# The join of block inverses in 64x64 array tiles over zeroed rows, with all steps in a new order

## The chip, the core and the metric

The kernel runs on one core of one Trainium2 chip. The metric is the device time of one execution in microseconds. The profile shows the core's engines: PE (TensorE, matrix products, with its weight loads as PEld), DVE (VectorE), ACT (ScalarE), POOL (GpSimd) and SP (which issues DMAs). Each engine works through its own queue in the order in which the program put the instructions there, and waits at an instruction until what it needs is done.

## The reference

A recurrent attention block (RWKV-7) on 4 batches, 8 heads, 768 steps and 40 dimensions feeds an exact GELU layer (3072 tokens, 320 to 2048 to 320):

```python
for t in range(S):
    y[:, :, t] = np.einsum('bhd,bhde->bhe', rt, state)
    Sa = np.einsum('bhde,bhe->bhd', state, at)
    state_decay = state * wt[:, :, None, :] - np.einsum('bhd,bhe->bhde', Sa, bt)
    state = state_decay + np.einsum('bhd,bhe->bhde', vt, kt)
...
h = x @ w_in
g = 0.5 * h * (1.0 + erf(h * inv_sqrt2))
return (g @ w_out).astype(np.float32)
```

The weights `w_in` and `w_out` come in float64 and are converted on the core.

## The kernel before, in words

The 768 steps are cut into 12 chunks `c` of 64 steps. There are 32 pairs of a batch and a head; two heads of 64 rows fill 128 partitions, and a state of 16 such units `n` is handled at once. Within a chunk the recurrence is solved with matrix products: the strictly triangular 64x64 matrix `N` of each unit has to be inverted (as I - N), and the inverse `Tt` is applied to the right-hand sides.

The inverse is made of blocks of 32 (`BL`). For chunk 0 it is done by repeated squaring on PE (`qm.0` to `qm.4`, with `qc`, `qz`, `qb`, `qa` on ACT and DVE between them); `qm.1` to `qm.4` multiply `both_ZT[half(q), n]`, 64 rows and 64 columns, into rows `half(q)`, where `half(q)` are the partitions 0 to 63 or 64 to 127. For the chunks 1 to 11 the two diagonal blocks are inverted on POOL: `nd` and `nx` bring the blocks into `Nb`, `iz` sets the start, `ic.c.j0.j1` does the elimination, step by step, with two POOL operations each (L961, L963), and `wx` (DVE, L932) brings the result into the right halves of the columns of `Tt`; `wa` (ACT, L937) copies the upper block's inverse to the left half. Then the two block inverses are joined by two products of 32x32 blocks: `tc_` transposes the upper block's inverse, `jm` multiplies it with the block of `N` between the two, `jc` (ACT, L1091) copies the result out of PSUM, `km` multiplies it with the lower block's inverse, and `kt0`, `kt1` (L1116) copy this into `Tt`. [...]

What uses the inverse: `av` and `xm` make the right-hand sides, `xc0`, `xc1` copy them, `sm` multiplies with `Tt`, `sc` masks, `pk` and `pb` make the products for the new state and the outputs, `oa`, `od`, `om` (DVE) add and scale them, `oc`, `ot`, `tn` turn the state for the next chunk, `ym` and `yc` use it there. `om` writes the rows of the chunk's output into `xt`, and `ox.c.0`, `ox.c.1` (DMA on SP's queue) move the rest of them across partitions. With `xt` complete, `mh.c.0` to `mh.c.7` are the products with `w_in` (L1309, 64x64 tiles, four of them in turn), `ge` the GELU, and for chunks 1 to 11 the second layer is done by seven products `m1` to `m7` with sums and differences `s1` to `s4`, `e1` to `e6` (a Strassen step; L1348). Other steps that the prediction names: `nm`, `am`, `vm` are the products that make `N` and its neighbours (L193, four 64x64 tiles), `cu` sums of logarithms, `sk` and `sb` scalings, `Ls` and `Lf` the loads of the weights, `warm` and `warm_first` products whose result nobody reads.

The order is written out by hand or by a search, in one string of step names in `order` (about 1450 of them): `perform` calls the steps in this order, and each step puts its instructions at the ends of the queues of its engines. So the string fixes the order in every queue, SP's with the DMAs too, and every wait follows from it. All matrix products that go through the helper `mm` carry its line, L193.

PSUM is held in four banks of [128, 2, 512]; `take` and `drop` hand them out in order.

Of the kernel before, what the change touches and what calls it, by code (L numbers as in the profile page):

```python
# [18 lines left out]
def order(chunks, first_seven):  # L19
    return """  # L20
        first_ones.1 Lw.1 stripes_set identity pads_extra.1 sums_mask Lw.0 pads_r.1 warm.4.20 upper_mask
        pads_extra.3 La.0 pads_a.1 warm.4.0 pads_VR.1 pads_VR.0 of_half_set Lb.0 bias_set warm.4.13 pads_r.0 lg.1
        first_ones.0 pads_w.0 pads_rows.0 warm.4.25 pads_extra.0 Lb.1 pads_rows.1 onward_set lg.0 pads_w.1 wT.1
        pads_a.0 pads_extra.2 La.1 wT.0 warm.4.2 ew.1 Lf.0.1.0 ta.0 Lf.1.1.0 cu.0 Lf.0.0.0 cu.1 ec.0 Lf.1.0.0
        ew.0 sb.0 tb.0 sa.0 Lk.0 warm.4.15 sn.0 ec.1 nm.0 sb.1 Lf.2.0.0 warm_set tb.1 nk.0 Lf5.0.0 ta.1 sn.1 qt
        parity_set iz.1 sa.1 qm.0 qi.0.p qi.1.v nm.1 qz.0 warm_first ce.1 Lf.3.0.0 nk.1 qb.0.0.v Lf.3.1.0 qc.0
        cs.1 qb.0.1.a nd.1 qm.1 sk.0.p ce.0 nx.1 Lr.0 cm.1 Tt_zero tk.0 cs.0 cn.1 ic.1.0.4 qc.1 Lf.2.1.0 cl.1
        cx.1 qz.1 kc.0 Lf5.0.1 qb.1.0.v qa.1 qb.1.1.a cm.0 cy.1 ic.1.4.8 qm.2 Lf.0.0.1 cv.0 ce.3 LV.0 warm.4.18
        qz.2 am.0 qb.2.0.v qa.2 cs.3 ic.1.8.12 tr.0 Lf.1.0.1 ce.2 ak.0 Lw.2 qb.2.1.a cs.2 qc.2 Lf.0.1.1 rc.0 qm.3
        Lk.1 ic.1.12.16 Lf.2.0.1 qa.3 qz.3 Lf5.1.1 tv.0 qb.3.0.v qb.3.1.a cm.3 cm.2 cv.3 qm.4 vc.0 ic.1.16.20  # L30
# [5 lines left out]
        mh.0.0 nk.2 ot.0.1 cg.6 ot.0.0 ak.1 Ls.1 nd.2 Ls.0 nx.2 mh.0.1 iz.2 ce.8 tn.0 LV.2 unused.a mh.0.2 wb.1
        cs.8 ic.2.0.4 Lk.2 cm.8 cv.8 ge.0.0 av.1 Ls.6 ce.11 ym.1 ce.10 cs.11 ic.2.4.8 Ls.5 mh.0.3 tc_.1 Lr.2
        cm.11 yc.1 sk.2.v xm.1 cs.10 Ls.7 ge.0.1 cm.10 tv.2 ic.2.8.12 Ls.9 xc1.1 cv.10 xc0.1 Ls.10 jm.1 vc.2
        cv.11 Ls.8 tr.2 ce.12 tk.2 Ls.11 mh.0.6 ce.13 cs.12 ic.2.12.16 La.3 cm.12 kc.2 cs.13 mh.0.7 wa.1.1 cm.13
        jc.1 cv.12 rc.2 am.2 vm.2 cv.13 ic.2.16.20 ce.14 pm.0.0 Ls.13 cl.14 cs.14 Ls.12 ce.15 cm.14 ak.2 Lw.3  # L40
        cn.14 cs.15 km.1 wa.1.0 cg.14 vk.2 pm.0.1 kt1.1 ta.3 kt0.1 Ls.15 cm.15 Ls.14 cv.15 ic.2.20.24 ce.16 Lbt.3
        sm.1 ge.0.3 cs.16 ce.17 mh.0.4 sc.1.0 Lwt.3 sc.1.1 cl.17 ic.2.24.28 cm.16 mh.0.5 cs.17 Lr.3 cm.17 lg.3
        cv.16 pk.1 cn.17 cg.17 pb.1 ge.0.2 oa.1.0 cu.3 Lk.3 oa.1.1 pm.0.3 ec.3 od.1.0 Lw.4 ic.2.28.31 od.1.1 oc.1
        tw.3 ot.1.0 om.1.1 sk.3.p ot.1.1 om.1.0 av.2 tn.1 ox.1.1 pc.0.1 lt.3 ym.2 wx.2 iz.3 pm.0.2 tc_.2 yc.2
        unused.r pw.3 so.0.1 ew.3 tb.3 ox.1.0 jm.2 wb.2 en.3 pc.0.0 xm.2 jc.2 sn.3 km.2 xc0.2 tr.3 mh.1.0 xc1.2
# [5 lines left out]
        tk.4 m7.1 ic.3.24.28 e4.1 LV.4 tb.4 m4.1 e5.1 Lr.5 ic.3.28.31 xm.3 e6.1 pw.4 so.1.1 mh.2.6 xc0.3 La.5
        wx.3 ew.4 tc_.3 cu.4 sb.3 jm.3 en.4 so.1.0 mh.2.7 wb.3 sn.4 Lv.4 wa.3.0 jc.3 xc1.3 wa.3.1 km.3 sa.4 ec.4
        mh.2.4 sk.4.p tr.5 ge.2.3 kt1.3 Lkt.5 iz.4 ta.5 kt0.3 nm.4 sm.3 nk.4 Lw.5 mh.2.5 nd.4 nx.4 sc.3.0
        ic.4.0.4 mh.2.2 sc.3.1 Lbt.5 tv.4 mh.2.3 ic.4.4.8 kc.4 Lb.4 pk.3 ge.2.1 Lwt.5 ge.2.2 tb.5 pb.3 mh.2.0
        ic.4.8.12 sb.4 oa.3.1 oa.3.0 mh.2.1 od.3.0 om.3.1 am.4 ge.2.0 ic.4.12.16 om.3.0 vm.4 od.3.1 ox.3.1 m1.2
        s1.2 lg.5 tw.5 oc.3 ot.3.0 m2.2 s2.2 s4.2 m5.2 Lv.5 e1.2 vk.4 lt.5 ic.4.16.20 ot.3.1 s3.2 m6.2 ox.3.0
        ak.4 pw.5 m3.2 e3.2 ew.5 m7.2 La.6 e2.2 ic.4.20.24 tn.3 en.5 e4.2 m4.2 e5.2 av.4 e6.2 tk.5 so.2.1
        ic.4.24.28 ym.4 sn.5 Lr.6 mh.3.6 yc.4 sa.5 tv.5 LV.5 xm.4 ic.4.28.31 cu.5 xc1.4 xc0.4 mh.3.7 ec.5 wx.4
        tc_.4 wa.4.1 iz.5 ta.6 nm.5 ge.3.3 vm.5 Lbt.6 tr.6 wb.4 jm.4 nk.5 mh.3.2 jc.4 nd.5 Lwt.6 wa.4.0 nx.5
        mh.3.3 kc.5 ic.5.0.4 Lkt.6 vk.5 km.4 ge.3.1 mh.3.0 kt1.4 ic.5.4.8 kt0.4 tb.6 La.7 am.5 sm.4 tw.6  # L60
# [1408 lines left out]
```

## Time and profile before

| | |
|---|---|
| median of 3 runs | 650.9 us (650.2 to 651.37) |
| the profiled execution | 648.82 us, span 646.9 us |
| PE busy | 617.4 us, 95% |
| DVE, POOL, ACT busy | 457.3, 379.6, 323.9 us |
| mean granted PE clock | 0.991 |

The span is from the first to the last instruction; some 2 us lie around it. "Busy" of PE is modelled, since its products are pipelined: the time that a group of products takes is better read from its start to the start of the next. A matrix product of the program appears as two records, each with its load of weights. A row of the profile gives the line, engine, operation, the tiles written and read, the array tile (rows*columns) and the size, the count, busy time and mean, and the idle time of the engine just before, with what ended it.

### The profile page before, as it was taken

What the parts mean: (1) busy time and instruction counts of PE and PEld (TensorE: products, weight loads), DVE (VectorE), ACT (ScalarE), POOL (GpSimd) and SP (SyncE); (2) the same over time, 40 slices, a digit from 0 to 9 for tenths busy, and PEclk for the clock granted to TensorE, in tenths of its full rate; (3) what the DMA queues carried; (4) which work ended last, traced back from release to release, by engine and by line L of the source; (5) the groups of instructions that cost most, each with busy time, mean ns of one, the idle gap of its engine ahead of it and who ended that gap; (6) DMA issues with size and microseconds to landing.
All of it is one profiled execution on the core that took longest, in us unless ns stands there. A gap on an engine that the chain in (4) does not pass through costs nothing.

```text
span 646.9 us, 31736 instructions
## 1 busy us (share of the span) xinstructions
PE 617.4 (95%) x14338; PEld 530.9 (82%) x14338; DVE 457.3 (71%) x557; ACT 323.9 (50%) x456; POOL 379.6 (59%) x782
## 2 busy tenths in 40 slices
PE   7798999989999999998999999999998999999997
PEld 4576886768988988977887998988986987989977
DVE  0889889869887987884977876975883874843313
ACT  4467797863462564733644436463572466042021
POOL 4388289707855857848948548858704867910000
PEclk9799999989999999999999999999999999999999
DMA  8998586757477358384538346348447124110100
GB/s 132 183 174 153 119 187 165 133 107 131 98 137 135 63 101 151 77 136 86 110 80 149 65 96 113 70 88 143 94 74 128 25 48 89 38 28 4 32 13 20
DMA packets 246914, 64.31 MB, mean 99 GB/s; under 512 B 228380, under 2 KB 243644, under 8 KB 246780
## 3 DMA queue, kind: packets, MB, share of 16 engines
q1 hardware_dynamic: 246340, 62.01, 51.2%
q8 instruction: 112, 1.84, 1.3%
q10 hardware_dynamic: 440, 0.29, 0.2%
q14 instruction: 22, 0.18, 0.1%
HBM read 54.39 MB, written 3.93 MB: 90 GB/s over the span
## 4 chain that ended last, share of the span: by engine, by line
PE 74%; issue 2%; ACT 2%; DVE 1%; DVEq 0%; ACTq 0%
PE bank L1309 29%; PE bank L1348 26%; PE bank L193 18%; DVE kT L721 0%; ACT L1314 0%; ACT L734 0%; ACT spare L922 0%; ACT T L942 0%; ACT Tt L937 0%; DVE spare L864 0%; ACT wpT L734 0%; ACT st L1194 0%; ACT kT L738 0%; ACT gt L1314 0%; DVE Tt L932 0%
## 5 line engine op out<-in xcount | busy, mean ns | idle before, releaser
L1309 PE MATMUL bank<-xt,w_in_sb 64*64 64x256 f32 x3840 | 224.5, 379 | 6.7 <-issue 6.0
L961 POOL TENSOR_TENSOR tmp<-W,Nb 128x126 f32<-128x126 f32 (+22 forms) x341 | 162.8, 478 | 95.3 <-DVE Nb L927 69.7
L1309 PEld LDWEIGHTS bank<-xt,w_in_sb 64*64 64x64 f32 x3840 | 161.3, 133 | 52.0 <-issue 11.1
L963 POOL TENSOR_TENSOR W<-W,tmp 128x126 f32<-128x126 f32 (+22 forms) x341 | 169.0, 496 | 26.7
L1348 PE MATMUL bank<-w_out_sb,gt 128*128 128x160 f32 x704 | 101.1, 301 | 0.0
L1314 ACT ACTIVATE gt<-bank 128x1024 f32<-128x1024 f32 x48 | 48.8, 1025 | 99.5 <-PE bank L1309 99.4
L1348 PEld LDWEIGHTS bank<-w_out_sb,gt 128*128 128x128 f32 x704 | 96.6, 190 | 2.3 <-issue 1.3
L1175 DVE TENSOR_TENSOR SM<-bank,upper 128x832 f32<-128x832 f32 (+1 forms) x24 | 23.0, 988 | 27.0 <-PE bank L193 25.8
L1263 ACT COPY conv<-st 32x128 f32<-32x128 f32 (+2 forms) x55 | 28.0, 510 | 17.6 <-DVE st L1257 15.9
L1227 DVE TENSOR_TENSOR st<-bank,st 128x832 f32<-128x832 f32 (+1 forms) x22 | 21.2, 986 | 14.4 <-PE bank L193 14.4
L1299 DVE TENSOR_TENSOR conv<-gt 128x1024 f32<-128x1024 f32 x11 | 14.1, 1280 | 24.3 <-ACT gt L1314 24.2
L1348 PE MATMUL bank<-extra,conv 128*128 128x160 f32 x208 | 30.3, 300 | 0.0
L1299 DVE TENSOR_TENSOR os<-os,bank 128x160 f32<-128x160 f32 x44 | 13.8, 314 | 21.8 <-PE bank L1348 20.1
L1348 PEld LDWEIGHTS bank<-extra,conv 128*128 128x128 f32 x208 | 28.9, 190 | 0.1
L721 DVE TENSOR_TENSOR_SCAN kT<-spare,kT 128x256 f32<-128x256 f32 x36 | 25.5, 766 | 0.8 <-ACT kT L714 0.7
L1348 PE MATMUL bank<-extra,gt 128*128 128x160 f32 x176 | 25.8, 300 | 0.0
L1348 PEld LDWEIGHTS bank<-extra,gt 128*128 128x128 f32 x176 | 24.5, 190 | 0.1
L789 POOL TENSOR_TENSOR bk_rows<-bk_rows,part 128x640 f32<-128x640 f32 x9 | 14.9, 1659 | 15.0 <-ACT part L742 13.4
L193 PE MATMUL bank<-SM,Tt 64*64 64x104 f32 (+1 forms) x768 | 20.6, 248 | 1.8 <-issue 1.5
L193 PEld LDWEIGHTS bank<-SM,Tt 64*64 64x64 f32 x768 | 19.0, 133 | 3.7 <-issue 2.3
L1314 ACT ACT_TABLE_LOAD x17 | 21.8, 1283 | 0.3
L1348 PE MATMUL bank<-extra,SM 128*128 128x160 f32 x144 | 21.2, 300 | 0.0
(220 smaller groups left out, 1117.5 us busy)
## 6 DMA issues: line engine op xcount, KB each, us to landing
bk_rows<-in_b_dram SPq DMA_DIRECT2D x24, 160.0 KB
bk_rows<-in_k_dram SPq DMA_DIRECT2D x24, 160.0 KB
out_dram<-os SPq DMA_DIRECT2D x46, 80.0 KB
VR<-in_v_dram SPq DMA_DIRECT2D x22, 160.0 KB
w_tile<-in_w_dram SPq DMA_DIRECT2D x36, 80.0 KB
a_pairs<-in_a_dram SPq DMA_DIRECT2D x18, 144.0 KB
a_pairs<-in_b_dram SPq DMA_DIRECT2D x18, 144.0 KB
v_pairs<-in_w_dram SPq DMA_DIRECT2D x18, 144.0 KB
```

The source lines that it names most:

```text
L193: nc.tensor.matmul(o, lhsT, rhs, start=first, stop=True, skip_group_check=True)
L721: nc.vector.tensor_tensor_scan(logs[:, at:at + n], onward, logs[:, at:at + n], 0.0, ALU.mult, ALU.add)
L789: (nc.vector if q == "v" else nc.gpsimd).tensor_tensor(to, rows(k_of(c)), decays(c), ALU.mult)
L961: nc.gpsimd.tensor_tensor(t, W[:, BL // 2 - rows:, rest:rest + 1].to_broadcast([P, rows, rest]), Nb[:, rest:rest + 1, :rest].to_broadcast( ...
L963: nc.gpsimd.tensor_tensor(own, own, t, ALU.add)
L1175: nc.vector.tensor_tensor(SM[:, g, :, :, cols], pair_of(f"S{c}_", g).rearrange("p x i c -> p i x c")[:, :, :, cols], kept, ALU.mult)
L1227: nc.vector.tensor_tensor(to, pair_of(f"QY{c}_", g)[:, :, :, cols], to, ALU.add)
L1263: nc.scalar.copy(apart.rearrange("p e i g d -> p (e i g) d")[to_rows, :, to_col:to_col + n], st.rearrange("p e i g c -> p (e i g) c")[rows ...
L1299: nc.vector.tensor_tensor(to, one_, other, how)
L1309: nc.tensor.matmul(ph[half(x ^ y), x, s], w_in_sb[half(x), kt, at:at + HP], xt[half(x), kt], start=kt == 0, stop=kt == NK - 1, skip_group_ ...
L1314: nc.scalar.activation(gt[:, 4 * q:4 * q + 4].rearrange("p (x s) t -> p x s t", x=2), bank(f"ph{c}_{q}").rearrange("p x (s t) -> p x s t", ...
L1348: nc.tensor.matmul(po[:, n, :DM // 2], l_[:, f], r_[:, f], start=f == 0, stop=f == NF // 2 - 1)
```

## The change

`jm` and `km` of the chunks 1 to 11 no longer use 32x32 tiles of the array. `jm` takes all 64 rows of a half: the 64x64 `N` of the unit against the transposed upper inverse, whose lower 32 rows are zero, since `tc_` now reads the left half of `Tt`, which is zero there. `jc` copies the lower blocks of the result, in two copies, into a `Js` tile whose other rows are zero (`Js_zero`, once). `km` takes 64 rows and 64 columns of `Js` (its own block and, without use, the next) against the right half of `Tt`. `wb` and `T2` go. The number of products stays, 32 a step.

```diff
     def tc_(c):
-        nc.vector.transpose(L_of(c), flat(Tt)[:, :, BL:] if c < NX else flat(Tt)[:, :, :BL])
+        nc.vector.transpose(L_tile, flat(Tt)[:, :, :BL])
...
     def jm(c):
-        J = take(f"J{c}")[:, 0].rearrange("p (n t) -> p n t", n=NBL)
-        for n in range(NBL):
-            for q in range(2):
-                mm(J[(lo if n % 2 else hi)[q], n // 2], N[lo[q], n, BL:], L_of(c)[lo[q], n])
+                    mm(join(f"J{c}")[half(q), n], N[half(q), n], L_tile[half(q), n])
...
-    def jc(c):
+    def jc(c, q):
-            nc.scalar.copy(Js_tile, J[:, :G * NP])
+            nc.scalar.copy(Js_tile[hi[q], :NBL], join(f"J{c}")[hi[q]])
...
     def km(c):
-                if n % 2:
-                    mm(J[lo[q], 1, n // 2], Js_tile[lo[q], n // 2], T2[lo[q], n // 2])
-                else:
-                    mm(J[lo[q], 0, n // 2], Js_tile[hi[q], n // 2], F[hi[q], n, BL:])
+                    mm(join(f"K{c}")[half(q), n], Js_tile[half(q), n:n + 2].rearrange("p n t -> p (n t)"),
+                       flat(Tt)[half(q), n, BL:])
...
-    def wb(c):
-        for x in range(2):
-            nc.scalar.copy(T2[lo[x]], flat(Tt)[hi[x], 1::2, BL:])
...
+    def Js_zero():
+        nc.gpsimd.memset(Js_tile, 0.0)
```

Beside it the whole string of `order` is another one: every step but `wb` is there, in a new place. PE has the same 354 steps in it, the ten `warm` and `warm_first` among them. The places that the prediction speaks of, first as they were, then as they are (steps between are left out):

```diff
-        first_ones.1 Lw.1 stripes_set identity pads_extra.1 sums_mask Lw.0 pads_r.1 warm.4.20 upper_mask
...
-        parity_set iz.1 sa.1 qm.0 qi.0.p qi.1.v nm.1 qz.0 warm_first ce.1 Lf.3.0.0 nk.1 qb.0.0.v Lf.3.1.0 qc.0
...
-        La.2 tv.1 om.0.1 om.0.0 Ls.2 cs.4 cm.4 Lf.3.0.1 vc.1 tr.1 od.0.1 cv.4 ox.0.0 am.1 rc.1 unused.v wT.2 ce.6
-        sb.2 warm.4.1 one_set od.0.0 wx.1 ew.2 ta.2 ox.0.1 tb.2 sa.2 vm.1 sn.2 cs.6 cl.6 cm.6 nm.2 vk.1 oc.0 cn.6
+        warm_set stripes_set warm_first Lw.0 pads_w.1 Lb.0 lg.0 pads_VR.0 identity sums_mask warm.4.1 upper_mask
+        warm.4.13 warm.4.20 first_ones.0 cu.0 pads_extra.0 ec.0 pads_w.0 wT.0 pads_a.0 ew.0 sb.0 tb.0 La.0 ta.0 Lw.1
...
+        Lf5.0.1 lg.2 cu.2 Lr.1 pb.0 od.0.0 ic.1.4.8 tr.1 Lf.1.0.1 ec.2 od.0.1 tv.1 om.0.0 om.0.1 Lf.1.1.1 cl.6 Lf5.0.0
...
+        ic.1.28.31 vc.1 vm.1 ox.0.1 tk.1 Ls.3 Ls.0 ot.0.0 Lf.3.0.1 ta.2 vk.1 sb.2 tb.2 ce.6 ew.2 kc.1 sn.2 am.1 cs.6
+        wx.1 ox.0.0 wa.1.0 sa.2 nm.2 Ls.2 cm.6 cn.6 Lk.2 cg.6 wa.1.1 ak.1 av.1 Ls.1 mh.0.0 mh.0.1 ot.0.1 nk.2 nd.2
...
+        ge.5.1 sc.6.1 mh.5.5 ge.5.2 ic.7.20.24 Lbt.8 ic.7.24.28 pk.6 pb.6 s1.5 s2.5 oa.6.1 od.6.1 oa.6.0 om.6.0 od.6.0
+        m1.5 m2.5 e1.5 sk.7.p oc.6 m5.5 e3.5 m6.5 tb.8 s3.5 m3.5 s4.5 ic.7.28.31 m7.5 ot.6.1 Lw.8 lg.8 wx.7 Lkt.8 iz.8
+        ot.6.0 tn.6 om.6.1 ew.8 e2.5 Lb.7 e4.5 ym.7 e5.5 LV.7 wa.7.1 av.7 wa.7.0 tc_.7 Lv.8 tv.8 yc.7 m4.5 e6.5 tk.8
```

The diff also removes steps that no order calls (`Ns`, `Nl`, `Is`, `If`, `Ij`), and moves the start pattern of `parity` from `Js` to `tmp`.

More of the change, by code (lines that the diff above doesn't have):

```diff
@@ L36, in order @@
[L36 to L45, printed above, removed]
@@ L51, in order @@
[L51 to L60, printed above, removed]
@@ L896, in ak @@
         masked(A_of(c).rearrange("p j g n t -> p j (g n) t"), f"A{c}")
-    @step
-    def Ns(c, j, q="s"):
-        N, blk = flat(N_of(c)), N_blocks[c % 2]
-        for z in range(2):
-            at = j * HP + z * BL
-            engine(q).dma_start(out=blk[j, z].rearrange("n s t -> s n t"),
-                                in_=N[at:at + BL, :, z * BL:(z + 1) * BL])
     Nb, W = (t.rearrange("p (s t) -> p s t", t=BL) for t in (Nb_tile, W_tile))
-    @step
-    def Nl(c, par, q="s"):
-        blk = N_blocks[c % 2].rearrange("j z n s t -> (j z n) s t")
-        engine(q).dma_start(out=Nb[half(par)], in_=blk)
     @step
@@ L939, in wb @@
     @step
-    def wb(c):
-        for x in range(2):
-            nc.scalar.copy(T2[lo[x]], flat(Tt)[hi[x], 1::2, BL:])
-    @step
     def iz(c):
         nc.gpsimd.memset(W, 0.0)
-        if c < NX:
-            for x in range(2):
-                nc.gpsimd.tensor_copy(W_tile[:, x::BL + 2], parity[:, x, :BL // 2])
-            return
-        for par in range(2):
-            nc.gpsimd.memset(W[half(par)].rearrange("p s t -> p (s t)")[:, par::BL + 2][:, :BL // 2], 1.0)
+        for x in range(2):
+            nc.gpsimd.tensor_copy(W_tile[:, x::BL + 2], parity[:, x, :BL // 2])
     @step
@@ L958, in ic @@
             t = tmp_tile[:, :rows * rest].rearrange("p (s t) -> p s t", s=rows)
-            if c < NX:
-                own = W[:, BL // 2 - rows:, :rest]
-                nc.gpsimd.tensor_tensor(t, W[:, BL // 2 - rows:, rest:rest + 1].to_broadcast([P, rows, rest]),
-                                        Nb[:, rest:rest + 1, :rest].to_broadcast([P, rows, rest]), ALU.mult)
-                nc.gpsimd.tensor_tensor(own, own, t, ALU.add)
-                continue
-            nc.gpsimd.tensor_tensor(t, W[:, :rows, j:j + 1].to_broadcast([P, rows, rest]),
-                                    Nb[:, j:j + 1, j + 1:].to_broadcast([P, rows, rest]), ALU.mult)
-            nc.gpsimd.tensor_tensor(W[:, :rows, j + 1:], W[:, :rows, j + 1:], t, ALU.add)
-    @step
-    def Is(c, par, q="s"):
-        rows = inv_blocks[c % 2].rearrange("j z n (s q) t -> q (j z n) s t", q=2)
-        engine(q).dma_start(out=rows[par], in_=W[half(par)])
-    @step
-    def If(c, j, q="s"):
-        inv = inv_blocks[c % 2]
-        for z in range(2):
-            at = j * HP + z * BL
-            engine(q).dma_start(out=flat(Tt)[at:at + BL, :, z * BL:(z + 1) * BL],
-                                in_=inv[j, z].rearrange("n s t -> s n t"))
-    @step
-    def Ij(c, j, q="s"):
-        engine(q).dma_start(out=T2[j * HP:j * HP + BL],
-                            in_=inv_blocks[c % 2][j, 1].rearrange("(n z) s t -> z s n t", z=2)[1])
+            own = W[:, BL // 2 - rows:, :rest]
+            nc.gpsimd.tensor_tensor(t, W[:, BL // 2 - rows:, rest:rest + 1].to_broadcast([P, rows, rest]),
+                                    Nb[:, rest:rest + 1, :rest].to_broadcast([P, rows, rest]), ALU.mult)
+            nc.gpsimd.tensor_tensor(own, own, t, ALU.add)
     lo = [slice(q * HP, q * HP + BL) for q in range(2)]
@@ L1059, in qx, with first_join, join @@
             nc.scalar.copy(flat(Tt)[rows, :, cols], T_[rows])
-    def L_of(c):
-        t = turned.rearrange("p g n t -> p (g n t)") if c < NX else convs[1].bitcast(FP32)
-        return t[:, :NBL * BL].rearrange("p (n t) -> p n t", t=BL)
+    L_tile = turned.rearrange("p g n t -> p (g n t)")[:, :NBL * BL].rearrange("p (n t) -> p n t", t=BL)
     @step
     def tc_(c):
-        nc.vector.transpose(L_of(c), flat(Tt)[:, :, BL:] if c < NX else flat(Tt)[:, :, :BL])
+        nc.vector.transpose(L_tile, flat(Tt)[:, :, :BL])
+    def first_join(name):
+        return bank(name).rearrange("p z (n t) -> p z n t", n=NBL)
+    def join(name):
+        return bank(name)[:, 0].rearrange("p (n t) -> p n t", n=NBL)
     @step
@@ L1095, in km @@
     def km(c):
[L1096 to L1103 removed]
+        take(f"K{c}", 2)
         for n in range(NBL):
             for q in range(2):
[L1106 to L1109 removed]
+                if c == 0:
+                    mm(first_join("K0")[lo[q], q, n], power_[hi[q], n], T_[hi[q], n])
+                else:
+                    mm(join(f"K{c}")[half(q), n], Js_tile[half(q), n:n + 2].rearrange("p n t -> p (n t)"),
+                       flat(Tt)[half(q), n, BL:])
     def kcopy(c, q, copy):
[L1112 to L1116 removed]
+        copy(flat(Tt)[lo[q], :, BL:], first_join("K0")[lo[q], q] if c == 0 else join(f"K{c}")[lo[q]])
+        drop(f"K{c}")
     @step
```

182 lines of the change are left out of this document (87 added, 95 removed).

## The prediction

> **What bounds the kernel now.** I read the page's busy times first, then the same by stage, then PE's waits, then PE's instructions in order of time. The first two rows of the page, and the four stages (columns: time, then busy us and instructions of PE, PEld, DVE, ACT, POOL, then clock, DMA share, GB/s):
>
> ```profile
> span 646.9 us, 31736 instructions
> PE 617.4 (95%) x14338; PEld 530.9 (82%) x14338; DVE 457.3 (71%) x557; ACT 323.9 (50%) x456; POOL 379.6 (59%) x782
> ...
> 0.00:76.77 76.77, 66.46 (x1594) 49.14 (x1598) 53.25 (x83) 46.76 (x62) 42.18 (x115) 0.96 0.88 152
> 76.77:137.00 60.23, 58.61 (x1350) 45.29 (x1340) 51.38 (x72) 51.45 (x71) 44.93 (x77) 1.00 0.71 148
> 137.00:600.00 463.00, 449.11 (x10901) 398.85 (x10902) 341.25 (x384) 219.21 (x315) 292.52 (x590) 1.00 0.49 92
> 600.00:646.90 46.90, 43.26 (x509) 37.62 (x507) 11.39 (x21) 6.53 (x11) 0.00 (x0) 0.99 0.09 23
> ```
>
> The first `mh` starts at 76.77. From there to 600 TensorE is busy 507.7 of 523.2 us (58.61 + 449.11 of 60.23 + 463.00), at full clock, and no other engine is near it. So in that stretch a step that takes TensorE longer costs what it adds, and a better order of the queues can win back no more than the idle 15.5 us. What the idle time is made of, by PE's waits (total us, times, longest):
>
> ```profile
> PE bank L193 <- issue: 10.1, 9, 2.2
> PE bank L1309 <- issue: 6.0, 8, 1.2
> ```
>
> 16.1 us end with "issue": TensorE waits for nothing but its own instructions. Four of these places, in order of time (start, duration, what, idle before in brackets):
>
> ```profile
> 25.46 0.55 PE L193 MATMUL bank<-N,st 32*32 32x32 f32 x24 [2.20 <-issue]
> ...
> 55.35 0.59 PE L193 MATMUL bank<-st,N 32*32 32x32 f32 x25 [0.98 <-issue]
> ...
> 395.64 3.67 PE L1309 MATMUL bank<-xt,w_in_sb 64*64 64x256 f32 x59 [1.01 <-issue]
> ...
> 490.27 0.18 PE L193 MATMUL bank<-T,Js 32*32 32x32 f32 x1 [1.67 <-issue]
> ```
>
> They stand in, or soon behind, steps of 32x32 products, which use up instructions fastest. The first two belong to chunk 0, whose 32x32 steps stay. The rest, 16.1 - 2.20 - 0.98 = 12.9 us, lies in chunks 1 to 11.
>
> **The change, part by part.**
>
> *The joins.* `jm` and `km` of chunks 1 to 11 are 22 steps of 32 products, two records each. What they take now is read from start to next start, since the ends are modelled:
>
> ```profile
> 486.44 0.75 PE L193 MATMUL bank<-turned,spare 32*32 32x32 f32 x64
> 487.12 1.16 PE L193 MATMUL bank<-aT,nT 40*64 40x64 f32 x64
> ...
> 582.12 0.22 PE L193 MATMUL bank<-Tt,Js 32*32 32x32 f32 x2
> ...
> 582.80 2.39 PE L1309 MATMUL bank<-xt,w_in_sb 64*64 64x256 f32 x40
> ```
>
> 0.68 us for `jm` (487.12 - 486.44) and 0.68 for `km` (582.80 - 582.12). Now the new form: contraction 64, 64 columns of weights, 32 moving columns, rows `half(q)` to rows `half(q)`. Only two of the four 64x64 tiles are used, those on the diagonal. The kernel has such steps already, the squarings `qm.1` to `qm.4` of chunk 0 at L1010; the last of them has just the new shape:
>
> ```profile
> 32.43 2.08 PE L193 MATMUL bank<-turned,st 64*64 64x64 f32 x64
> 34.44 1.09 PE L751 MATMUL bank<-ident,extra 128*128 128x128 f32 x8
> ...
> 46.89 1.99 PE L193 MATMUL bank<-turned,st 64*64 64x32 f32 x61 [0.33 <-ACT st L1043]
> ...
> 510.55 1.16 PE L193 MATMUL bank<-aT,kT 40*64 40x64 f32 x64
> 511.53 1.11 PE L193 MATMUL bank<-rT,late 40*64 40x64 f32 x64
> ```
>
> `qm.1` takes 2.01 us (34.44 - 32.43) for 64 records, and 32 moving columns instead of 64 save nothing (1.99). A step over all four 64x64 tiles takes 0.98 (511.53 - 510.55): half, so the two tiles set the rate. I take 2.00 as it is the same shape and the same pair of tiles; the other end is 0.98. The term: 22 x (2.00 - 0.68) = **+29.0 us**, all on TensorE in the saturated stretch (lower end 22 x 0.30 = 6.6). [...]
>
> *The stalls.* The longest beside the 1.67 above:
>
> ```profile
> 296.50 0.21 PE L193 MATMUL bank<-T,Js 32*32 32x32 f32 x2 [1.65 <-issue]
> ```
>
> A slower join gives the instruction supply 1.3 us more. Of the stalls behind chunk 0 only these two exceed that. If each shrinks by 1.32, the two leave 0.35 and 0.33, the others nothing: 12.9 - 0.7 = **-12.2 us**. Ends: 0 (the stalls come from elsewhere) and -12.9 (all gone).
>
> *The copies.* Five of ACT's groups (busy us, mean ns, idle before) and a wait of POOL:
>
> ```profile
> L942 ACT COPY T<-Tt 32x256 f32<-32x256 f32 x22 | 8.9, 402 | 17.8 <-DVE Tt L932 17.4
> L1116 ACT COPY Tt<-bank 32x512 f32<-32x512 f32 x13 | 7.5, 574 | 13.6 <-DVE Tt L1116 9.6 <-issue 2.0 <-PE bank L193 1.8
> L1091 ACT COPY Js<-bank 128x256 f32<-128x256 f32 x11 | 4.0, 365 | 7.6 <-PE bank L193 7.5
> L937 ACT COPY Tt<-Tt 32x512 f32<-32x512 f32 x22 | 13.5, 614 | 0.8 <-DVE Tt L932 0.5
> L1314 ACT ACT_TABLE_LOAD x17 | 21.8, 1283 | 0.3
> POOL tmp L961 <- DVE Nb L927: 69.7, 9, 20.0
> ```
>
> `wb` (L942) goes, 22 copies of 402 ns; `jc` becomes two copies of 32 partitions, like L1116 at 574, for one of 365; ACT gains and loses 0.8 us a chunk, which nothing feels while it is busy 219 of 463. `tc_` now reads what `wa` wrote, so the path from `wx` to `kt` grows by two copies of 614, by 0.8 in `jc`, and by 2.6 in the products: 4.7 us a chunk. Its cover is the slack of POOL, which waits 69.7 us for the next block matrix; if that cover were gone, 11 x 4.7 = 52 us would show. I take zero.
>
> *The new order, before the first `mh`.* The same 354 steps stand on PE, so in the saturated stretch the order moves work and removes none. Only the first 76.77 us can gain or lose by it.
>
> ```profile
> 2.71 6.13 PE L193 MATMUL bank<-cum_m,ident 128*128 128x512 f32 x8 [2.71 <-POOL cum_m L360]
> 8.77 1.16 PE L193 MATMUL bank<-cum_m,SM 64*64 64x64 f32 x64
> ...
> 27.85 4.65 PE L193 MATMUL bank<-w_in_sb 128*128 128x512 f32 x6
> ```
>
> and two rows of SP, one of DVE, at the hand-over from chunk 0 to `mh.0`:
>
> ```profile
> 68.84 0.49 DVE L1257 TENSOR_TENSOR st<-bank,wpT 128x320 f32<-128x320 f32 x1
> 66.44 0.60 SPq L537 DMA_DIRECT2D gt<-in_moe_w_in_dram  x1
> 75.98 3.05 SPq L577 DMA_DIRECT2D w_out_sb<-in_moe_w_out_dram  x4
> ```
>
> `warm_first` leaves the place ahead of `qm.1`: -4.6 (32.43 - 27.85). It now leads the queue; 12 filler records at 0.76 (8 in 8.77 - 2.71) from about 1.3 us end near 10.4 where the first sums started at 8.77: +1.7. Behind `pb.0`, `od.0` now stands ahead of `om.0` (two of 0.49, +1.0), and on SP's queue five weight loads stand between the halves of the hand-over `ox.0` to `mh.0`, where none stood: 3.05 + 0.60 of issuing, +3.7. Net **+1.8**, between -2.9 (the later delays hidden) and +6.4 (the gain lost).
>
> *Further on*, the loads that the order moves go through SP's queue, and the DMA engines are half idle (0.49); nine more function tables on ACT at 1.28 us go into its idle half. I take zero; the end of an order that makes waits is the rival below.
>
> Sum: 29.0 - 12.2 + 1.8 = +18.6 on the profiled execution, 648.82 us with its span of 646.9, so 667.4. The median of the runs, 650.9, lies 2.1 above it; the forecast is on that: **669.5 us**.
>
> **The rivals.**
>
> *The stalls stay.* If the "issue" time belongs to places in the program and not to speed, nothing comes back: 650.9 + 29.0 + 1.8 = 681.7. Against it: only dense stretches show such stalls. For it: 395.64 lies inside `mh`, not in a join. [...]
>
> *Waits that the order makes.* In the new DVE queue `wx.7` stands ahead of `tn.6` and `om.6.1`. The rows that tell its slack, POOL's two and three of PE:
>
> ```profile
> L961 POOL TENSOR_TENSOR tmp<-W,Nb 128x126 f32<-128x126 f32 (+22 forms) x341 | 162.8, 478 | 95.3 <-DVE Nb L927 69.7
> L963 POOL TENSOR_TENSOR W<-W,tmp 128x126 f32<-128x126 f32 (+22 forms) x341 | 169.0, 496 | 26.7
> ...
> 500.87 1.61 PE L193 MATMUL bank<-VR,bk_rows 64*64 64x104 f32 x64
> 502.30 1.61 PE L193 MATMUL bank<-SM,bk_rows 64*64 64x104 f32 x64
> ...
> 610.35 17.50 PE L1309 MATMUL bank<-xt,w_in_sb 64*64 64x256 f32 x320
> ```
>
> Between `nx.7` and the end of `pb.6` the new PE order has seven `mh` of 2.18 (17.43/8 to the next start), `sm`, `pk`, `pb` of 1.43, two joins of 2.0, `am` of 0.98 and `cu`: 25 us; DVE then has some 9 us of operations ahead of `wx.7`: 34 in all. POOL needs (162.8 + 169.0)/11 = 30.2, with `sk.7` and `nx.7` about 33. One us of slack: 2 us late in six chunks would be +12, 681. For it: the slack; against: PE has `ym`, `av`, `m4`, `jm`, `vm` and `xm`, 9 us, ahead of the first `mh.6`.
>
> *Faster.* The squarings lie in the stage where DMA is busy 0.88 of the time; if that slowed them, and two tiles keep the pace of four, a join step costs 0.98: 6.6 - 12.2 + 1.8 = -3.8, 647.1. It decides once a step takes less than 0.68 + 10.4/22 = 1.15 us. Against it: 2.01 and 1.99 at `qm.1` and `qm.4`, 15 us apart, are too equal for a disturbance. That the joins stay as they were is excluded: the built program has 64x32 outputs there.
>
> **How the numbers follow.** Forecast 0.66; stalls stay 0.13; waits 0.13; faster 0.06; within 0.2% (1.3 us, about what this measurement can tell) 0.02. The range leaves out the faster case and the worst ends: low is all stalls gone (-12.9), a start of -2.9 and a join step of 1.7 us, between the two ends (22.4): 650.9 + 6.6 = 657; high is the two slower rivals with the worst start, 681.7 + 4.6 = 686.
>
> **What would show it.** `jm` and `km` as 64*64 64x32 with about 2.0 us from start to next start; PE's "issue" idle behind chunk 0 near 1 us; the first `mh` between 74 and 83 us; PE busy above 97% until the last chunk. The prediction is wrong if a join step takes near 1 us, if "issue" stays above 10, or if `mh.0` starts 10 us earlier.

## The result and the profile after

The changed kernel takes 679.1 us (median of 4 runs, 678.25 to 681.43) where the kernel before took 650.55 on the same chip: a ratio of 1.0451 with a 95% interval of 1.0412 to 1.0490, 29 us slower. The forecast was 669.5 us in a range of 657 to 686. The profiled execution took 678.82 us.

The first row of the page after, and three stages of it with three short windows (columns: time, busy us and instructions of PE, PEld, DVE, ACT, POOL, then clock, DMA share, GB/s). The stages are cut at the first `mh` and at the first `mh` of the last chunk.

```profile
span 677.0 us, 31760 instructions
...
0.00:82.44 82.44, 68.97 (x1659) 52.05 (x1663) 58.92 (x86) 54.63 (x74) 45.47 (x114) 0.96 0.84 144
82.44:639.45 557.01, 542.70 (x12256) 490.76 (x12248) 391.61 (x455) 274.14 (x371) 328.52 (x670) 0.98 0.49 93
639.45:677.00 37.55, 33.27 (x433) 31.93 (x432) 8.42 (x17) 7.53 (x10) 0.00 (x0) 0.99 0.09 21
188.30:195.10 6.80, 6.32 (x94) 6.23 (x98) 5.82 (x7) 2.60 (x4) 3.19 (x4) 0.50 0.57 94
239.50:242.90 3.40, 3.40 (x15) 3.40 (x14) 0.00 (x0) 0.00 (x0) 2.85 (x8) 0.50 0.13 28
451.10:457.90 6.80, 6.24 (x108) 4.44 (x112) 6.76 (x8) 4.01 (x6) 2.92 (x4) 0.50 0.81 151
```

The same cut of the kernel before, with one short window:

```profile
76.77:610.35 533.58, 518.07 (x12326) 454.32 (x12317) 395.52 (x459) 271.03 (x386) 337.45 (x667) 1.00 0.51 97
610.35:646.90 36.55, 32.91 (x433) 27.44 (x432) 8.51 (x16) 6.16 (x9) 0.00 (x0) 0.99 0.08 20
...
137.34:140.76 3.42, 2.92 (x84) 2.14 (x88) 3.20 (x3) 3.35 (x7) 0.00 (x0) 0.50 0.81 160
```

So the start grew by 5.7 us (82.44 - 76.77; 1.5 of it is `av.1`, which is now done ahead of the first `mh`), the long middle by 23.4 (557.01 - 533.58), the end by 1.0. The three short windows show what grew in the middle: the granted clock stands at 0.50 for stretches of 3.4 or 6.8 us, 17 us in all. The kernel before has one such stretch there, 3.4 us from 137.34 on; the rounded 1.00 of its row, and the prediction's "at full clock", hide it.

PE's waits of the kernel after (total us, times, longest), and its instructions at the joins of chunk 1 and at four waits:

```profile
PE bank L187 <- DVE aT L770: 5.4, 2, 3.9
PE bank L1284 <- ACT os L1329: 4.9, 3, 4.1
PE bank L187 <- DVE turned L1014: 4.4, 1, 4.4
PE bank L187 <- issue: 2.4, 3, 1.2
```

```profile
78.24 1.34 PE L187 MATMUL bank<-aT,nT 40*64 40x64 f32 x64 [3.92 <-DVE aT L770]
...
96.80 2.01 PE L187 MATMUL bank<-turned,spare 64*64 64x32 f32 x64
98.74 1.97 PE L187 MATMUL bank<-ident,VR 128*64 128x128 f32 x32
...
105.73 2.00 PE L187 MATMUL bank<-Tt,Js 64*64 64x32 f32 x64
107.67 2.69 PE L1366 MATMUL bank<-w_out_sb,gt 128*128 128x320 f32 x9
...
188.78 3.52 PE L187 MATMUL bank<-turned,spare 64*64 64x32 f32 x62 [4.37 <-DVE turned L1014]
...
238.85 4.04 PE L1284 MATMUL bank<-extra,SM 128*128 128x160 f32 x16 [4.13 <-ACT os L1329]
...
449.79 0.41 PE L187 MATMUL bank<-st,aT 40*64 40x104 f32 x8 [1.23 <-issue]
451.66 1.99 PE L187 MATMUL bank<-aT,nT 40*64 40x64 f32 x64 [1.46 <-DVE os L1235]
```

A join step takes 1.94 us here (98.74 - 96.80, 107.67 - 105.73) instead of 0.68. Most later ones take less: at 510.93 a join starts, at 512.66 the `mh` behind it, and at 512.71 the join's last two records. From record to record, the 21 at full clock take 1.80 us in the median and 1.83 in the mean, so that the 22 add some 25 us, not the 27.7 of the figures below, which go by chunk 1. "Issue" fell from 16.1 to 2.4 us, and only 1.23 of it lies behind chunk 0. In its place stand waits for other engines: nm.2 (3.92), jm.3 (4.37), m6.2 (4.13), nm.9 (1.46). Rows of DVE and of ACT for three of them:

```profile
76.27 0.71 DVE L913 STREAM_TRANSPOSE Tt<-W 128x512 f32<-128x512 f32 x1 [3.37 <-POOL W L934]
76.91 1.19 DVE L770 TENSOR_TENSOR aT<-bank,wpT 128x1024 f32<-128x1024 f32 x1
...
185.35 0.71 DVE L913 STREAM_TRANSPOSE Tt<-W 128x512 f32<-128x512 f32 x1 [6.67 <-POOL W L934]
```

```profile
235.08 1.28 ACT L731 ACT_TABLE_LOAD   x1 [0.81 <-DVE kT L718]
...
237.56 1.06 ACT L735 ACTIVATE kT<-kT 128x1024 f32<-128x1024 f32 x1
238.52 0.27 ACT L1329 COPY os<-bank 128x160 f32<-128x160 f32 x1
```

On DVE `sa.2` (L770), which nm.2 needs, stands behind `wx.1` (L913), which waits 3.37 us for POOL; `wx.3` waits 6.67 us for POOL and jm.3 waits for it. On ACT the copy `e3.2` of 0.27 us (L1329), which frees m6.2's bank, stands behind the exponentials `ew.5` and `en.5`, which wait 0.81 us for a scan on DVE and then take 3.4 us themselves (235.08 to 238.52).

**Where the stalls stand.** The idle time in the profile is counted from the modelled end of a product. From start to start a stall is some 0.2 to 0.4 us longer, and one thing becomes visible in it. If all instructions of PE's queue are numbered (products, weight loads, semaphore instructions), the "issue" stalls of the kernel before of 0.5 us and more stand in front of these:

```
number           705 1985 4545 6337 8641 10945 11457 12993 13505 16065 17345 18113 19905 20673 22465 25025
(number-193)/256   2    7   17   24   33    42    44    50    52    62    67    70    77    80    87    97
```

Every one is 193 more than a multiple of 256. Its waits for other engines stand at other remainders, and the "issue" stalls of all later kernels here have the same 193. So PE's instructions come in blocks of 256, and PE stalls, as the packets below show, where a block was used up before the next was there. A step of 64 records is 128 instructions, half a block; a join of 0.68 us beside a product step of 0.98 makes a block of 1.66 us.

The page of the kernel before lists what brings these blocks, among its DMA queues (packets, MB, share):

```profile
q8 instruction: 112, 1.84, 1.3%
```

112 packets of 16 KiB for the 28795 instructions of PE's queue are one packet for each block of 256. The trace has their times. At chunk 5's stall a block begins at 292.88, the packet of the next starts at 293.95 and has landed at 295.16, and the next block begins at 296.50. All 17 stalls behind the first `mh` end 1.3 to 1.7 us behind the landing of their packet, and in none of the kernels here does a block begin less than 1.19 us behind its own. So what PE waits for at these places is its instructions.

From the first `mh` on, counted from start to start and above 0.3 us, the kernel before has 17 such stalls with 18.4 us of its span of 646.9, the one after 2 with 2.0 us of 677.0.

### The profile page after: what moved, and what is told of

It is laid out like the page before. It is cut to its first block, busy times and chain, and to the rows that moved or that the text cites. A ratio compares the mean times of both kernels' runs of the same rounds, so it can differ in the third digit from the quotient of the medians.

```text
span 677.0 us, 31760 instructions
## 1 busy us (share of the span) xinstructions
PE 644.9 (95%) x14338; PEld 574.7 (85%) x14338; DVE 458.9 (68%) x557; ACT 336.3 (50%) x454; POOL 374.0 (55%) x783
## 4 chain that ended last, share of the span: by engine, by line
PE 75%; POOL 9%; SPq 7%; DVE 3%; issue 2%; DMA 1%; ACT 1%; DVEq 0%; POOLq 0%; ACTq 0%
PE bank L1245 28%; PE bank L1284 23%; PE bank L187 22%; POOL W L934 5%; POOL tmp L932 4%; SPq L444 2%; PE bank L1366 2%; SPq L534 2%; SPq L1184 1%; SPq L452 1%; DMA gt<-in_moe_w_in_dram 1%; DMA r_pairs<-in_k_dram 0%; SPq L1181 0%; DMA a_pairs<-in_a_dram 0%; DVE kT L718 0%
## 5 line engine op out<-in xcount | busy, mean ns | idle before, releaser
L932 POOL TENSOR_TENSOR tmp<-W,Nb 128x126 f32<-128x126 f32 (+22 forms) x341 | 161.1, 472 | 155.9 <-DVE Nb L908 130.4
L1245 PEld LDWEIGHTS bank<-xt,w_in_sb 64*64 64x64 f32 x3840 | 173.8, 135 | 31.5 <-issue 2.7
L934 POOL TENSOR_TENSOR W<-W,tmp 128x126 f32<-128x126 f32 (+22 forms) x341 | 163.1, 478 | 26.7
L1199 ACT COPY conv<-st 32x128 f32<-32x128 f32 (+2 forms) x55 | 28.1, 511 | 14.3 <-DVE st L1193 13.6
L1111 DVE TENSOR_TENSOR SM<-bank,upper 128x832 f32<-128x832 f32 (+1 forms) x24 | 22.8, 991 | 12.2 <-PE bank L187 12.2
L1053 DVE COPY Tt<-bank 32x512 f32<-32x512 f32 x10 | 6.9, 689 | 32.6 <-ACT Tt L1053 15.3
L1284 PE MATMUL bank<-extra,SM 128*128 128x160 f32 x144 | 23.2, 317 | 4.9 <-ACT os L1329 4.9
L718 DVE TENSOR_TENSOR_SCAN kT<-spare,kT 128x256 f32<-128x256 f32 x36 | 27.4, 819 | 0.0
L918 ACT COPY Tt<-Tt 32x512 f32<-32x512 f32 x22 | 13.5, 614 | 27.3 <-DVE Tt L913 27.1
L1284 PEld LDWEIGHTS bank<-extra,SM 128*128 128x128 f32 x144 | 21.3, 201 | 5.8 <-ACT os L1329 5.6
L1038 ACT COPY Js<-bank 32x512 f32<-32x512 f32 x22 | 12.7, 577 | 27.2 <-PE bank L187 27.0
```

The costliest lines, as they stand in the source:

```text
L718: nc.vector.tensor_tensor_scan(logs[:, at:at + n], onward, logs[:, at:at + n], 0.0, ALU.mult, ALU.add)
L932: nc.gpsimd.tensor_tensor(t, W[:, BL // 2 - rows:, rest:rest + 1].to_broadcast([P, rows, rest]), Nb[:, rest:rest + 1, :rest].to_broadcast( ...
L934: nc.gpsimd.tensor_tensor(own, own, t, ALU.add)
L1111: nc.vector.tensor_tensor(SM[:, g, :, :, cols], pair_of(f"S{c}_", g).rearrange("p x i c -> p i x c")[:, :, :, cols], kept, ALU.mult)
L1199: nc.scalar.copy(apart.rearrange("p e i g d -> p (e i g) d")[to_rows, :, to_col:to_col + n], st.rearrange("p e i g c -> p (e i g) c")[rows ...
L1245: nc.tensor.matmul(ph[half(x ^ y), x, s], w_in_sb[half(x), kt, at:at + HP], xt[half(x), kt], start=kt == 0, stop=kt == NK - 1, skip_group_ ...
```

## The experiments

My theory: the joins cost 27.7 us and give the stalls back by their slowness; the rest of the 29 us is the new order, by waits of PE and the half clock behind them. The rivals: the new order removed the stalls (then the joins cost their full price and the order nothing), or the waits are not the order's.

### The joins alone, the order alone

Old order, new joins (the order string of before, with `wb` gone and `wa` behind `wx`; here chunk 7, the others alike):

```diff
-wx.7 tc_.7 iz.8
+wx.7 wa.7.0 wa.7.1 tc_.7 iz.8
...
-jc.7 pw.9 wb.7 mh.6.0
+jc.7.0 jc.7.1 pw.9 mh.6.0
```

> The old order with the joins in 64x64 tiles (the copies of the upper inverse right behind `wx`). If a join step costs 1.94 instead of 0.68 us and gives the "issue" stalls back by its slowness (my theory), the joins alone cost 22 x 1.26 = 27.7 less 11.7: 650.6 + 16.0 = 666.6 us, with "issue" behind chunk 0 below 2 us. If the stalls went because of the new order and not of the joins, they stay here near 12.9 us and the time is 650.6 + 27.7 = 678.3. If the joins also make waits of their own (two more copies on the path from `wx` to `jm`), it is above 667 with "issue" low and waits of PE for `turned` (L1014).

Measured: 664.7 us, ratio 1.0237 (1.0192 to 1.0281), which on 650.6 is +15.4. PE's waits and the middle stage:

```profile
PE bank L186 <- issue: 3.5, 4, 1.9
...
PE bank L186 <- ACT Js L1037: 2.4, 6, 1.0
PE bank L186 <- DVE turned L1013: 2.2, 2, 1.9
PE bank L1244 <- issue: 1.3, 2, 0.9
```

```profile
76.99:626.19 549.20, 541.07 (x12328) 496.74 (x12319) 394.62 (x459) 270.74 (x372) 336.86 (x667) 0.99 0.50 94
```

"Issue" is 4.8 us in all. With the old order and only slower joins the stalls are nearly gone: from start to start 4 of 3.2 us are left of 17 of 18.4. The theory's time (666.6) holds, inside 663.1 to 668.9 by the interval, and the rival's (678.3) falls. The new copies show too: one wait of 1.9 us for `turned`, and small ones for `Js`.

New order, old joins (`wb` put back behind `jm`):

```diff
-jm.7 jc.7.1 jc.7.0 vm.8
+jm.7 wb.7 jc.7 vm.8
```

> The new order with the joins in 32x32 tiles as before (`wb` behind `jm`). If the order costs waits of its own and the joins heal the stalls (my theory), the order alone costs 679.1 - 666.6 = 12.5: about 663 us, with "issue" stalls near 13 us again, PE's waits for `aT` (L770), `os` (L1329) and `turned` (L1014) as in the changed kernel, and a lower clock behind them. If the order itself removed the stalls, and the joins cost their full 27.7, it is 679.1 - 27.7 = 651.4 with "issue" below 3 us.

Measured: 666.8 us, ratio 1.0274 (1.0240 to 1.0309), +17.8.

```profile
PE bank L187 <- DVE aT L767: 5.5, 2, 3.9
PE bank L1342 <- ACT os L1387: 5.4, 3, 4.6
PE bank L187 <- issue: 5.2, 6, 1.6
PE bank L187 <- DVE turned L1061: 4.4, 1, 4.4
...
82.09:625.59 543.50, 521.87 (x12256) 445.92 (x12248) 391.81 (x455) 274.82 (x383) 330.11 (x669) 0.98 0.50 95
```

The same waits as in the changed kernel stand here without its joins, so they are the order's. But my theory was half wrong as well: the stalls did not come back. From start to start there are 3 of 3.2 us. Part of it is that the new order has fewer short blocks (behind the first `mh`, 25 of 99 last under 4 us with the stalls taken out, against 40 in the kernel before), part may be that PE's waits give the next block time, which is not shown apart. Either edit alone removes most of the stalls, and they can be won only once.

Worked out from the spans of the profiled executions (joins: 22 x 1.26; stalls from start to start; the start less 1.5 for `av.1`; the rest is what is left, that is new waits and half clock; with 25 for the joins it is some 2 us more in the first and the last row):

| against before | joins | stalls | start | end | rest | span |
|---|---|---|---|---|---|---|
| joins alone | +27.7 | -15.2 | +0.2 | +0.1 | +3.1 | +15.9 |
| order alone | 0 | -15.2 | +3.8 | +1.2 | +26.6 | +16.4 |
| both (the change) | +27.7 | -16.4 | +4.2 | +1.0 | +13.6 | +30.1 |

The two single rows add up to 32.3, near the 30.1 of both, but not because the edits are independent: 14.0 us of stalls are counted twice in that sum, and the rest is 16.1 smaller for both (13.6) than in the two rows (29.7). The second fits that a PE which needs 27 us more waits less for the others; no run shows it by itself. The sum of a trace's stalls holds to some 4 us only: the run with one copy moved, further below, has PE's order of before and 14.8 us instead of 18.4. The rest, by subtraction, holds no better.

### The waits of the new order

One wait mended, in the changed kernel:

```diff
-ew.5 en.5 s4.2 m5.2 so.1.1 e3.2 e2.2
+s4.2 m5.2 so.1.1 e3.2 ew.5 en.5 e2.2
```

> The changed kernel with one wait mended: `e3.2` ahead of `ew.5` and `en.5` on ACT, so that m6.2 needn't wait 4.13 us. If a long wait of PE costs its own length and a stretch of 3.41 us at half clock behind it (1.7 us), it is 5.8 us faster than the changed kernel, 673; if it costs its length alone, 675; if what follows is late anyway, 679.

Measured: ratio 1.0370 (1.0336 to 1.0404), 5.3 us less than the changed kernel's (the intervals do not meet); the span is 3.0 us less. m6.2 and the window around it, first in this kernel, then in the changed one:

```profile
236.34 2.44 PE L1283 MATMUL bank<-extra,SM 128*128 128x160 f32 x16 [0.38 <-ACT os L1328]
...
230.00:245.00 15.00, 14.62 (x296) 13.97 (x299) 13.97 (x15) 8.99 (x14) 13.59 (x19) 1.00 0.49 101
```

```profile
230.00:245.00 15.00, 10.87 (x177) 10.56 (x170) 10.62 (x12) 6.79 (x12) 13.35 (x22) 0.89 0.55 111
```

The wait fell from 4.13 to 0.38, and with it went the stretch at half clock. That the wait was the order's is shown. Whether it costs its length or also the 1.7 us behind it, 3.0 to 5.3 us can't tell.

Four waits mended:

```diff
-wx.1 ox.0.0 wa.1.0 sa.2 nm.2
+sa.2 wx.1 ox.0.0 wa.1.0 nm.2
...
-mh.2.6 jm.3 jc.3.1 mh.2.7 xc1.3 jc.3.0 Lv.4 pw.4 km.3
+mh.2.6 mh.2.7 m3.1 jm.3 jc.3.1 xc1.3 jc.3.0 Lv.4 pw.4 m4.1 km.3
...
-wx.8 m4.6 ox.7.0 vm.9 e6.6
+m4.6 ox.7.0 vm.9 e6.6 wx.8
```

(and the edit above)

> The changed kernel with four of its long PE waits mended in the order: `sa.2` ahead of `wx.1` (nm.2 waited 3.92), `mh.2.7`, `m3.1` ahead of `jm.3` and `m4.1` ahead of `km.3` (jm.3 waited 4.37), `e3.2` ahead of `ew.5`, `en.5` (m6.2 waited 4.13), `wx.8` behind `e6.6` (nm.9 waited 1.46). If these waits, and the half clock that stands behind each of them, are the price of the new order, 13.9 us of waiting go and up to 20.5 us at half clock behind them (10 us): 679 comes down to that of the joins alone, about 665, or a little below. If the waits only move to another place because POOL's chain is the bound, it stays above 674.

Measured: 673.1 us, ratio 1.0343 (1.0305 to 1.0382): 7.0 us less than the changed kernel's, not 14, and 1.7 us less than with the one wait mended, which the two intervals can't tell from nothing.

```profile
PE bank L186 <- DVE late L860: 3.0, 1, 3.0
...
PE bank L1244 <- ACT SM L1089: 2.4, 1, 2.4
PE bank L186 <- DVE aT L772: 2.1, 1, 2.1
```

The four waits are gone and others came: nm.2 no longer waits, but the step behind it waits 3.0 us for `late`, and elsewhere stand new waits of 2.1 and 2.4 us. Of the 14 us between the changed kernel and the joins alone, half is mended; the new waits, 7.5 us together, are about the other half. Both theories were too simple here.

### What sets the rate of a join

Two 32x32 tiles instead of four, old order:

```diff
-mm(J[(lo if n % 2 else hi)[q], n // 2], N[lo[q], n, BL:], L_of(c)[lo[q], n])
+mm(J[hi[q], n], N[lo[q], n, BL:], L_of(c)[lo[q], n])
```

(`km` likewise from `hi` rows alone, without `T2` and `wb`)

> The old order with the joins still in 32x32 tiles, but on two of the array's tiles instead of four (all products of a half write the same rows; `wb` goes). If the number of tiles in use sets the rate, a join step takes near 1.3 us, costs 22 x 0.65 = 14 and takes away most of the stalls (1.3 us less each, some 9 us of them): 650.6 + 5 = about 656 us. If the products are paced by their number alone, a step stays at 0.68 and the time at 650.6, with the stalls. If the stalls are not healed by pace but by the form 64x64, it is 650.6 + 14 = 665.

Four 64x64 tiles instead of two, old order:

```diff
-mm(join(f"J{c}")[half(q), n], N[half(q), n], L_tile[half(q), n])
+mm(spread(f"J{c}", n % 2)[half(q ^ n % 2), n // 2], N[half(q), n], L_tile[half(q), n])
```

(`km` likewise; `spread` takes the other bank of the pair for odd `n`, and the copies take each half back)

> The old order with the joins in 64x64 tiles, but spread over all four of them: the products of odd units write the other half's rows, in the other bank of the pair, and four copies a join take them back. If two tiles set the rate of 1.94 us, a step here takes 0.98 us: against the kernel with the joins alone 22 x 0.96 = 21.1 less, with some of the stalls back (each may be 0.95 us longer, some 7 us of the 12.9): 666.6 - 21.1 + 7 = 652 us. If the tile's size, the 64 columns of weights, sets the rate, it stays at 666.

Measured: 651.4 us, 1.0042 (1.0018 to 1.0066), and 654.2 us, 1.0079 (1.0044 to 1.0114). The steps, first on two small tiles, then on four large ones:

```profile
484.82 1.20 PE L186 MATMUL bank<-turned,spare 32*32 32x32 f32 x64
485.95 1.16 PE L186 MATMUL bank<-aT,nT 40*64 40x64 f32 x64
```

```profile
488.40 1.08 PE L186 MATMUL bank<-turned,spare 64*64 64x32 f32 x64
489.31 1.14 PE L186 MATMUL bank<-aT,nT 40*64 40x64 f32 x64
...
PE bank L186 <- ACT Js L1041: 5.2, 7, 2.1
```

1.13 us on two small tiles, 0.91 on four large ones, against 0.68 on four small and 1.94 on two large. So the number of tiles in use sets the rate, for the large ones by a factor of about 2, for the small ones of 1.7 (1.13/0.68); the size counts too, with 1.6 to 1.7 on two tiles (1.80 to 1.94 against 1.13) and 1.3 on four (0.91/0.68). Stalls from start to start: 9.8 us at 1.13, 7.8 at 0.91, 3.2 at 1.94, 18.4 at 0.68. On two small tiles the sum closes: 22 x 0.45 = 9.9 less 8.6 of stalls is 1.3, and 0.42% is 2.7 us. In the old order the joins of the change cost 0.8% instead of 2.4% on all four tiles. There 22 x 0.23 = 5.1 (some 7 with the `km` steps, which take 1.05 in the median) less 10.6 of stalls would be a gain; PE's 5.2 us of waits for the copies of `Js`, where it was 1.5, take a part of it.

### Even blocks of instructions

A first try moved 38 of the `mh` steps by one or two places, chosen by the lengths of the blocks alone. Three of them (mh.2.1, mh.7.0, mh.7.1) came to stand behind a write of the next chunk's rows into `xt`, and so multiply other rows; the work is as much as before. One of the moves:

```diff
-mh.6.7 kc.8 ic.8.0.4 Lw.8 vm.8 ge.6.3 am.8
+kc.8 ic.8.0.4 Lw.8 vm.8 mh.6.7 am.8 ge.6.3
```

> The kernel before, joins and all as they were, with 38 of its `mh` steps moved by one or two steps of PE from chunk 2 on, so that no block of 256 records of PE's queue (counted so that the stalls in the traces stand at its borders) is left with only small products. If the "issue" stalls come from blocks that PE empties faster than the next is there, they fall from 12.9 us behind chunk 0 to some 4 and the time to 648.5 - 8 = about 640 us. If they belong to something else, "issue" stays near 13 and the time at 648.5. If the moved products make waits of their own, the time is above 650 with "issue" low.

Measured: ratio 1.0606 (1.0555 to 1.0658).

```profile
PE bank L187 <- issue: 7.4, 11, 2.0
PE bank L187 <- DVE aT L770: 6.1, 1, 6.1
```

A third outcome: fewer stalls, many new waits. An `mh` moved back brings the small steps behind it forward by 2.2 us, before their inputs are there. The next try moved only six, all forward, each ahead of one small step with room behind it:

```diff
-km.5 wa.5.0 tw.7 sk.5.p mh.4.3
+mh.4.3 km.5 wa.5.0 tw.7 sk.5.p
...
-jm.7 ic.8.4.8 wa.7.1 tw.9 mh.6.4
+mh.6.4 jm.7 ic.8.4.8 wa.7.1 tw.9
```

(and four like these)

> The kernel before with six `mh` steps each moved ahead of one small step (`mh.4.3` ahead of `km.5`, `mh.8.1` of `km.9`, `mh.3.2` of `jm.4`, `mh.6.4` of `jm.7`, `mh.7.6` of `am.9`, `mh.9.0` of `km.10`). In the trace of before, the stalls of chunk 5 (1.79), 9 (1.81), 4 (1.00), 7 (1.33), 9 (1.37) and 10 (1.05) each stand behind a block of 256 instructions of PE's queue that lasts 1.7 to 3.3 us; the moves make these six blocks 2.6 to 4.3 us long. If a block that is used up too fast is what stalls, these six stalls, 8.35 us, shrink by 1.7 + 0.95 + 1.0 + 0.8 + 0.9 + 1.05 = 6.4: about 644 us, and the other stalls stay. If the stalls have another cause, 650. If the small steps that now come 2.2 us later are waited for, above 650 with "issue" low.

Measured: 645.1 us, ratio 0.9933 (0.9902 to 0.9963): 0.7% faster than the kernel before. PE around chunk 5's first join and chunk 9's, and one stall elsewhere:

```profile
248.88 2.39 PE L1303 MATMUL bank<-xt,w_in_sb 64*64 64x256 f32 x40 [1.37 <-issue]
...
292.56 0.75 PE L187 MATMUL bank<-turned,spare 32*32 32x32 f32 x64
293.25 1.16 PE L187 MATMUL bank<-aT,kT 40*64 40x64 f32 x64
294.23 2.34 PE L1303 MATMUL bank<-xt,w_in_sb 64*64 64x256 f32 x40
...
485.85 1.45 PE L1303 MATMUL bank<-xt,w_in_sb 64*64 64x256 f32 x18 [1.01 <-issue]
```

Where the kernel before stalled 1.65 us in km.5, nothing stalls. Of the six stalls, that of chunk 5 is gone; that in chunk 9's km went from 1.67 to 1.01 and now falls into the `mh` ahead of it; three are smaller, one block earlier or later, and that of chunk 4 came back longer (1.37 at 248.88, where it was 0.67). From start to start the six fall from 8.6 us to 4.6, less than the 6.4 expected. All stalls fall from 18.4 to 12.9, but not by the moves alone: the run with one copy moved has 14.8 with no move, that with both edits 15.6 with all six, and the six places, each with a block to either side, have 8.5 and 6.8 in these two. So the moves took some 2 to 4 us of stalls. The time fell by 4.4 us in the ratio; the granted clock, too, is 1.00 here from chunk 0 to the end. This bears out, with the joins untouched, what the packets show; how long a single stall is it can't foretell.

One copy moved on ACT:

```diff
-en.3 pc.0.0 xm.2 jc.2
+jc.2 en.3 pc.0.0 xm.2
```

> The kernel before with `jc.2` on ACT ahead of `en.3`, so that km.2 (which waited 1.53 us for it) needs to wait 1.04 us less. If a wait of PE of this size draws a stretch of 3.41 us at half clock behind it, the time falls by 1.0 + 1.7, to about 647.8; if it costs its length alone, 649.5 (hardly to be told from 650.5); if what follows waits in its place, no change.

Measured: ratio 1.0027 (0.9998 to 1.0056).

```profile
136.69 0.22 PE L187 MATMUL bank<-Tt,Js 32*32 32x32 f32 x2 [0.58 <-ACT Js L1085]
...
141.39 1.16 PE L187 MATMUL bank<-aT,nT 40*64 40x64 f32 x64 [1.62 <-DVE aT L770]
```

km.2 waits 0.95 us less, and nm.3 behind it now waits 1.62: the wait went one step on, and nothing is won. The half clock at 137.34 went with it, but two stretches of 3.4 us stand elsewhere instead, from 294.72 and 489.28 on, at "issue" stalls of 1.91 and 2.32 us.

> Both of the foregoing edits of the kernel before. If they add, 650.5 - 6.4 - 2.7 = about 641 us, faster than either kernel; if the stalls stay, 648; if the moved products are waited for, above 650.

Both edits together measured 0.9952 (0.9923 to 0.9981): not the 641 us of the sum; within the intervals the gain of the six moves, and nothing from the copy.

## Why the prediction was right or wrong

The direction and the range held; the forecast was 10 us too low, and the 679 us lie nearer to the two slower rivals (681.7 and 681) than to it. The range held because its upper end was taken from these rivals, not from the forecast's own terms.

- **The joins, +29.0.** Right in mechanism, a little high: 1.94 us a step at chunk 1 (22 x 1.26 = 27.7), 1.80 in the median, some 25 us in all. The squarings on the same two tiles gave the price, and the runs with two small and four large tiles show why it was theirs: half the tiles cost a factor of 1.7 to 2, the larger size one of 1.3 to 1.7.
- **The stalls, -12.2.** Right in mechanism and in size: "issue" behind chunk 0 went from 12.9 to 1.2. The joins alone do it, so "the stalls stay" falls. From start to start the gain is 16.4, since idle time is counted from modelled ends. The packets show the supply that the step named. What it did not see: the new order alone removes most of them as well.
- **The copies, 0.** Nearly: in the joins alone PE waits 1.9 us once for `turned` and 2.4 in all for `Js` (1.5 before).
- **The start, +1.8.** Too low: the first `mh` starts at 82.44, 5.7 later, at the upper end. The listed terms left out `av.1`, now ahead of it (1.5), and `sa.2` behind `wx.1`, which makes nm.2 wait 3.92; with it mended, and a new wait of 3.0 in its place, `mh` starts at 79.54.
- **The order in the saturated stretch, 0.** This step failed. "The order moves work and removes none" is true of work and says nothing of waits: by subtraction, waits and half clock cost 13.6 us there (some 16 by the joins' mean) with the new joins, 26.6 without them. The rival *Waits that the order makes* had the right kind and nearly the price (+12), but named `wx.7` ahead of `tn.6` and `om.6.1`; PE's long waits stand at nm.2, jm.3, m6.2 and nm.9 instead, so that the prices agree is chance. The string could have been read for them: a short copy that frees a bank (`e3.2`) behind two long exponentials, an operation that PE needs (`sa.2`) behind a transposition that waits for POOL's last step.
- **PE busy above 97%** came true (542.70 of 557.01) and said nothing, since products at half clock count as busy (3.40 of 3.40 us in the window at 0.50 from 239.50 on). The clock column (0.98 for 1.00) was the sign to name.
- **Faster, 647.1.** Rightly small: two tiles do not keep the pace of four, with 1.94 us a step at chunk 1. Four large tiles take 0.91 us a step, and even these end at 1.0079. Its sum was wrong beside that: it took the full 12.2 of stalls for a step only 0.30 us longer, where four large tiles, 0.23 us longer, leave 7.8 of 18.4.

## What to carry to other kernels

Price a step by the number of array tiles that it keeps busy (here 1.80 to 1.94 us on two 64x64 tiles, 0.91 on four), and look at how many instructions it needs per microsecond: where PE's queue has short steps side by side, a slower step or a long one between them can cost less than its length, because the stall at the block's border goes (the joins alone: 25 to 27.7 us more on PE, 15.2 us of stalls gone, 15.4 us slower). Two edits that remove the same stall are not to be added (joins and order take 15.2 us of stalls each, together 16.4). An order is to be searched queue by queue for a short instruction behind a long one or one that waits for another engine (here a copy of 0.27 us behind 3.4 us of exponentials, and `sa.2` behind a wait of 3.37), and mending one such wait may only show the next (0.95 us less at km.2, 1.62 at nm.3).

## What the runs showed that I had not expected

- PE's "issue" stalls stand only at borders of 256 instructions, in every kernel here, in the kernel before behind blocks of 1.8 to 4.0 us from start to start. Not each such block stalls, and the same border (145 us) stalled 1.0 us in one kernel and 1.8 in another. Part of it is the packet: at the 17 stalls it starts 0.6 to 2.2 us behind the border before and takes 0.9 to 1.4 us. Why its start varies stays open.
- At idle times of PE the granted clock fell to 0.50 for 3.4 or 6.8 us: at jm.3's wait of 4.37, behind m6.2's 4.13, but also at 451.1, between an "issue" stall of 1.23 and a wait of 1.46, and at "issue" stalls alone (1.91 and 2.32, above). Not each such wait has a stretch: km.2's of 1.53 has one in the kernel before (from 137.34 on) and none in that with the six moves. What decides it is not shown.
